# Retention by chunks of 64 tokens in every block, with two 64x64 products per output, in a retention-plus-maxout kernel on one core

## The chip, the cores and the metric

The kernel runs on one core of a Trainium2 chip. The core has a matrix engine (TensorE, PE in the profile; its weight loads are listed apart as PEld), VectorE (DVE), ScalarE (ACT), GpSimd (POOL) and the queue SP, which here issues nearly all DMAs. The engines run on their own and wait for each other by semaphores. The metric is the device time of one execution in microseconds; lower is better. The kernel before was timed three times: 755.7, 756.7 and 758.22 us, a median of 756.7 us.

## The reference

Two stages. The first is a causal retention over 8 batches, 8 heads, 576 tokens and 64 values per head; the second a feed-forward with three up-projections, of which the elementwise largest is kept, and one down-projection.

```python
scores = scale * np.matmul(q, k.transpose(0, 1, 3, 2))          # scale = 1/sqrt(64)
gamma = 1.0 - 2.0 ** (-5.0 - np.arange(H))
Dmat = np.where(rel >= 0, gamma ** rel, 0.0)                    # rel = query position - key position
attn = np.matmul(scores * Dmat, v)                              # (8, 8, 576, 64), per batch and head
x = attn.transpose(0, 2, 1, 3).reshape(4608, 512)
h = np.maximum(np.maximum(x @ w1, x @ w2), x @ w3)              # (4608, 768)
out = h @ w_out                                                 # (4608, 512), float32
```

q, k and v are float32; the four weights arrive as float64 and the kernel turns them into float32 itself.

## The kernel before, in words

The 4608 tokens are 36 *blocks* of 128 tokens (g = 0..35), and four blocks make a *tile* of 512 tokens (t = 0..8). While the feed-forward of tile t runs on TensorE, the retention of the four blocks of tile t+1 is put between its matmuls. A block has two *chunks* of 64 tokens; a batch has nine chunks (`place(g, c)` is 0 to 8).

Because gamma^(i-j) = gamma^i * gamma^-j, the decay is split: keys or values are multiplied by gamma^-j (`gk`), outputs by gamma^i/8 (`gq`), and what older tokens contribute is kept as a *state*, the sum of k^T v over them, multiplied by `gs` = gamma^128 from block to block.

*Blocks 0 to 7 (`BY_CHUNKS = 8`)* are done 128 tokens at once. `transposes` makes q^T and k^T (blocks 0 to 6 on TensorE, L285, with one ACT copy of 128x512 each, L286; block 7 on VectorE). `decay` multiplies v by `gk` on GpSimd into `vd` (L253). `scores` forms 8 products of 64 rows against 128x128 outputs (L299) and masks them with two DVE products (L302, reported as L198). `state` forms k^T v (L366) and `keep` adds it to the state. `values` forms 8 products of scores with values over 128 rows (L407) and 8 of state with q over 64 rows (L420), and `output` multiplies by `gq` into `xT`.

*Blocks 8 to 35* are done by chunks. `chunk_scores` forms, per head, up to four 64x64 products, one in each quadrant of the matrix engine: k^T v of each chunk (L317) and the scores of each chunk (L321). Scores and state lie stacked over the 128 partitions: for a chunk, `ms` holds the weights in one half and q^T in the other, `vas` holds the values in one half and the state in the other. So `chunk_values` needs one product over 128 rows per head and chunk (L438). For that stacking, the mask is two DVE products of 64x512 (L325, with `gm`, the causal mask times `gk`), half of q^T is copied on ACT (L313), and k is multiplied by `gk` on ACT, eight 128x64 products per block (L257, reported as L186). The new state is added on DVE (`keep_chunk`, L333) and multiplied by `gs` on GpSimd (L335).

*The feed-forward.* Tile 0 is plain: 18 up-projections (`up_plain`, L790, 4 matmuls of 512 columns each) and 24 down matmuls (`downs_plain`, L777). During tile 0 the weights arrive by DMA as 64-bit words and are converted in steps on DVE and ACT (`convert_all`, L637 to L663); one call of `convert(1)` runs one step. The very first up-projection is cut into 384 and 128 columns, so that its first part does not need block 3. Later tiles replace the ups by 20 products of 256 columns over sums of weights and of x (`up`, L766), the downs by 7 (`downs`, L564).

*What orders the work.* Instructions are issued in the order of the program text on each engine. `steps(t)` lists by hand at which of 12 points of a tile which step of which block is issued (`transposes`, `scores`, `decay`, `values`, `load`). From tile 1 on, DVE work is not issued at once but put in `urgent` (by `soon`) and handed out between matmuls by `chore`; ACT's scaling is handed out by `scale`. `scores` and `values` first issue all that is left of these. All loads stand in the one queue SP, in program order, and a load into a buffer waits for the last reader of what the buffer held. PSUM has eight banks: four for retention (`ps_r`, four buffers of one bank), two for `ps_x`, two for `ps_y`.

*The start (L869 to L912).* Blocks 0 to 3 are loaded; between them two small loads of `gs` (L874), and the first weight pieces behind block 3's q. Then transposes, scores, state and values of blocks 0 to 3 are issued one after the other, and after them the first up-projection.

## Time and profile before

| | |
|---|---|
| median of the three timed runs | 756.7 us |
| the profiled execution | 756.22 us |
| its span, first to last instruction | 754.5 us |
| PE busy | 745.1 us (99%) |
| DVE busy | 529.2 us (70%) |
| ACT busy | 336.3 us (45%) |
| POOL busy | 90.9 us (12%) |
| granted TensorE clock, mean | 1.000 |
| first up-projection starts | 25.36 us |
| tile 0 runs on PE (up and down) | 25.36 to 125.10 us |
| one later tile, from `e` to the next `e` | 208.57 to 287.37 us |

In the profile's tables a row names the line, the engine, the operation, output and inputs, their shapes, how often it occurs, busy time and the mean of one instruction. Matmuls overlap: the mean of one is not the time that a further one costs. What a stretch of matmuls costs is read from the timeline, from its first start to the start of what follows. Each float32 product appears as two records. A few records can be missing from a trace.

### The profile page before, as it was taken

To read this page: it belongs to the slowest core of one execution; us is meant where nothing else is said; L and a number is where in the kernel's file an instruction comes from. 1 tells how busy PE (TensorE), PEld (TensorE's weight loads), DVE (VectorE), ACT (ScalarE), POOL (GpSimd) and SP (SyncE) were. 2 spreads that over 40 slices of the span, in tenths; PEclk is the share of its full clock that TensorE was granted. 3 is DMA by queue.
4 is the path that set the end of the run, shared out by engine and by line. 5 is a ranking of instruction groups with operands and counts; after the bars stand their busy time and mean duration, and the time that the engine had idled before them with its cause. 6 is when DMAs were issued, how large, how long until landed. Compare 5 with 4: busy or idle time off the path is not lost.

```text
span 754.5 us, 15014 instructions
## 1 busy us (share of the span) xinstructions
PE 745.1 (99%) x5928; PEld 607.9 (81%) x5928; DVE 529.2 (70%) x879; ACT 336.3 (45%) x670; POOL 90.9 (12%) x112
## 2 busy tenths in 40 slices
PE   8999999999999999999999999999999999999998
PEld 7645545588888888888888888888888888888887
DVE  2998796958886866687567847685768666863662
ACT  3665531155245533553355435542555255414441
POOL 3210012002010110011010102010101010100000
PEclk9999999999999999999999999999999999999999
DMA  9995762504242414242343225242425141000001
GB/s 211 229 244 121 201 140 68 102 1 75 67 101 41 85 43 102 54 74 54 71 85 65 62 60 95 38 77 63 82 40 98 43 91 37 1 30 28 2 1 56
DMA packets 230310, 59.20 MB, mean 78 GB/s; under 512 B 211168, under 2 KB 228960, under 8 KB 230240
## 3 DMA queue, kind: packets, MB, share of 16 engines
q1 hardware_dynamic: 229664, 57.91, 35.5%
q8 instruction: 46, 0.75, 0.4%
q10 hardware_dynamic: 576, 0.33, 0.2%
q14 instruction: 24, 0.20, 0.1%
HBM read 48.76 MB, written 9.44 MB: 77 GB/s over the span
## 4 chain that ended last, share of the span: by engine, by line
PE 89%; DVE 5%; DMA 3%; SPq 1%; issue 1%; ACT 1%; DVEq 0%
PE a L766 18%; PE b L766 15%; PE dx L564 11%; PE c L766 8%; PE up L790 6%; PE dz L564 5%; PE d L766 5%; PE e L766 5%; PE o L438 4%; PE sk L317 3%; PE dy L564 3%; PE down L777 2%; DMA bits<-in_moe_w_out_dram 1%; PE sk L321 1%; SPq L247 1%
## 5 line engine op out<-in xcount | busy, mean ns | idle before, releaser
L754 DVE TENSOR_TENSOR part<-part 128x512 f32<-128x512 f32 x161 | 111.4, 692 | 93.6 <-ACT part L751 91.2
L751 ACT COPY part<-b 128x512 f32<-128x512 f32 x115 | 67.3, 585 | 140.2 <-PE b L766 140.2
L754 DVE TENSOR_TENSOR h<-h,part 128x512 f32<-128x512 f32 x115 | 79.6, 692 | 28.8 <-ACT h L751 24.6
L790 PE MATMUL up<-xT,w 128*128 128x512 f32 (+2 forms) x200 | 84.8, 579 | 1.0 <-DVE w L663 0.9
L751 ACT COPY part<-a 128x512 f32<-128x512 f32 x92 | 53.9, 585 | 48.9 <-PE a L766 48.4
L790 PEld LDWEIGHTS up<-xT,w 128*128 128x128 f32 x200 | 36.8, 190 | 43.3 <-issue 40.1
L766 PE MATMUL a<-s,w 128*128 128x256 f32 x276 | 70.9, 379 | 0.0
L766 PE MATMUL b<-s,n 128*128 128x256 f32 x276 | 70.8, 379 | 0.0
L186 ACT ACTIVATE kraw<-kraw,gk 128x64 f32<-128x64 f32 x208 | 65.6, 346 | 3.2 <-DMA kraw<-in_k_dram 2.9
L766 PEld LDWEIGHTS b<-s,n 128*128 128x128 f32 x276 | 52.4, 190 | 7.1
L766 PEld LDWEIGHTS a<-s,w 128*128 128x128 f32 x276 | 52.4, 190 | 7.2
L534 POOL TENSOR_TENSOR H<-h 128x256 f32<-128x256 f32 x24 | 20.2, 842 | 285.6 <-DVE h L754 285.5
L335 POOL TENSOR_TENSOR va<-va,gs_of 64x512 f32<-64x512 f32 x24 | 25.8, 1074 | 229.8 <-DVE va L333 184.2
L766 PE MATMUL c<-xT,w 128*128 128x256 f32 x184 | 49.1, 389 | 0.0
L766 PE MATMUL d<-s,w 128*128 128x256 f32 x184 | 47.3, 379 | 0.0
L766 PE MATMUL b<-xT,n 128*128 128x256 f32 x184 | 47.2, 379 | 0.0
L564 PE MATMUL dx<-To,H 128*128 128x256 f32 (+1 forms) x204 | 44.9, 370 | 0.0
L766 PE MATMUL e<-xT,w 128*128 128x256 f32 x184 | 43.5, 379 | 0.0
L766 PE MATMUL a<-xT,n 128*128 128x256 f32 x184 | 43.5, 379 | 0.0
L564 PEld LDWEIGHTS dx<-To,H 128*128 128x128 f32 x204 | 36.6, 190 | 4.9
L325 DVE TENSOR_TENSOR m<-sk,gm 64x512 f32<-64x512 f32 x56 | 38.5, 687 | 1.0
L766 PEld LDWEIGHTS e<-xT,w 128*128 128x128 f32 x184 | 35.0, 190 | 5.2 <-DVE va L331 0.2
(122 smaller groups left out, 1318.1 us busy)
## 6 DMA issues: line engine op xcount, KB each, us to landing
bits<-in_moe_w_dram SPq DMA_DIRECT2D x36, 256.0 KB, 5.5
out_dram<-osb SPq DMA_DIRECT2D x35, 256.0 KB, 2.1
kraw<-in_k_dram SPq DMA_DIRECT2D x32, 256.0 KB, 3.1
qraw<-in_q_dram SPq DMA_DIRECT2D x224, 32.0 KB, 2.2
kxraw<-in_k_dram SPq DMA_DIRECT2D x224, 32.0 KB, 2.1
va<-in_v_dram SPq DMA_DIRECT2D x56, 128.0 KB, 3.1
bits<-in_moe_w_out_dram SPq DMA_DIRECT2D x6, 512.0 KB, 6.3
vraw<-in_v_dram SPq DMA_DIRECT2D x7, 256.0 KB, 4.5
```

What stands on the lines that cost most here:

```text
L186: scaling.popleft()()
L317: nc.tensor.matmul(sk[c][half(c), h, :], lhsT=kr[half(c), h, :], rhs=vas[g, c][half(c), h, :], start=True, stop=True)
L325: nc.vector.tensor_tensor(ms[g, c][half(c)], sk[1 - c][half(c)], gm[half(c)], op=ALU.mult)
L335: nc.gpsimd.tensor_tensor(to[half(1)], to[half(1)], gs_of[half(1)].unsqueeze(2).to_broadcast([D, H, D]), op=ALU.mult)
L438: nc.tensor.matmul(o[half(c), n % 2, n // 2, half(m)], lhsT=vas[g, m][:, h, :], rhs=ms[g, m][:, h, :], start=m == 0 and n == 0, stop=True, ...
L534: urgent.append(lambda: (pool(s3, a11, a21, op=ALU.subtract), pool(s4, a12, s2, op=ALU.subtract)))
L564: nc.tensor.matmul(o, lhsT=hS[n](fp)[:, m * P:(m + 1) * P], rhs=late["T"][n][:, fp, cols], start=first and fp == order[0] and (m == 0 or l ...
L751: nc.scalar.copy(of[step], ps[step[0]][:])
L754: nc.vector.tensor_tensor(of[dst], a, b, op=op)
L766: nc.tensor.matmul(ps[chain][:, e, :], lhsT=factor(w, 2 * fp + e), rhs=xS[t][x], start=n == 1 and e == 0, stop=ends, skip_group_check=True)
L777: nc.tensor.matmul(b[:], lhsT=h[:, fb, m * P:(m + 1) * P], rhs=w_sb["out", fb], start=(fb == 0), stop=(fb == NF - 1))
L790: nc.tensor.matmul(ps[:, cols], lhsT=w_sb[i, fb][:, dc * P:(dc + 1) * P], rhs=xT[t][:, dc, cols], start=dc == 0 and cols.start == 0, stop= ...
```

## The change

Every block is done by chunks, and the stacked form is given up.

- `transposes` writes q^T and k^T so that chunk c lies in half c of the partitions. For blocks 0 to 6 (still transposed on TensorE) this takes four ACT copies of 64x256 per tensor instead of one of 128x512.
- `decay` multiplies v in place by `gk`: on VectorE for blocks 0 to 3, on GpSimd for the others until tile 1, then on ACT in eight pieces. k is not multiplied any more, and the mask is the bare causal mask, applied by one DVE product of 128x512 per block.
- `scores` forms scores and k^T v as before per head in four 64x64 quadrants, now into one tile of two PSUM banks: the scores of both chunks in the first, k^T v in the second. `keep_chunk` adds the states, one 64x512 DVE product per chunk.
- `values` takes two 64-row products per head and chunk, weights with values and then state with q^T, in the order (rows 0, out 0), (1, 1), (0, 1), (1, 0), which add up in PSUM. A pair of blocks shares one output tile of two banks.
- `ps_r` becomes two buffers of two banks. The helpers for blocks 0 to 7 (`state`, `keep`, `output`, `carry`, `state_factors`, `key_masks`) go, as does ACT's copy of half of q^T.
- The start: `gs` is loaded from ACT's queue ahead of everything else, `gq` in four DMAs on ACT's queue instead of two; the first weight pieces are loaded ahead of block 3. Blocks 0 to 2 are done first; `first_ups` runs the first up-projection over blocks 0 to 2 and the second over blocks 0 and 1, and does scores and values of block 3 between these parts. The transposes and scores of block 4 come one step later than before. In the last unit of tile 0 the maximum is issued ahead of the conversion steps.
- `FILL`, an unused tile, goes from 160 to 192 bytes per partition.

```diff
-    ps_r = ctx.enter_context(tc.tile_pool(name="ps_r", bufs=4, space=PSUM))
+    ps_r = ctx.enter_context(tc.tile_pool(name="ps_r", bufs=2, space=PSUM))
...
     nc.scalar.dma_start(gk[:], key_decay)
+    for j in range(2):
+        nc.scalar.dma_start(gs[0:D, j::2].unsqueeze(2), state_decay[D * j:D * (j + 1), :, D * j:D * j + 1])
...
-    def decay(g):
+    def decay(g, engine=nc.gpsimd):
+        t = vs[g]
         if spread:
+            scaling.extend(partial(nc.scalar.mul, t[:, h, :], t[:, h, :], gk[:, h:h + 1]) for h in range(H))
         else:
+            engine.tensor_tensor(t[:], t[:], gk[:].unsqueeze(2).to_broadcast([C, H, D]), op=ALU.mult)
...
+        for e, (n, src) in enumerate((("k", raws["k", g]), ("q", raws.pop(("q", g))))):
...
             for p in range(NP):
                 nc.tensor.transpose(pt[:, p, :], pair(src, p), ident[:C, :C])
-            nc.scalar.copy(both[n][:], pt[:])
+            for j in range(2):
+                for c in range(2):
+                    nc.scalar.copy(both[n][half(c), j::2, :], pt[half(j), :, half(c)])
...
     def scores(g):
         chore(len(urgent))
         scale(len(scaling))
+        qT, kT, kr = qks[g]["q"], qks[g]["k"], raws.pop(("k", g))
+        sk = ps_r.tile([P, 2, H, D], FP32, tag="r", name="sk")
+        kept = [c for c in range(2) if place(g, c) < CS - 1]
         for h in range(H):
             for c in range(2):
+                nc.tensor.matmul(sk[half(c), 0, h, :], lhsT=kT[half(c), h, :], rhs=qT[half(c), h, :],
                                  start=True, stop=True)
+            for c in kept:
+                nc.tensor.matmul(sk[half(1 - c), 1, h, :], lhsT=kr[half(c), h, :], rhs=vs[g][half(c), h, :],
+                                 start=True, stop=True)
+
+        def mask():
+            nc.vector.tensor_tensor(weights[g][:], sk[:, 0], lower, op=ALU.mult)
+
+        def keep_chunk(c):
+            r = half(1 - c)
+            new, kv = states[g + c][r], sk[r, 1]
+            factor = gs[r].unsqueeze(2).to_broadcast([D, H, D])
+            if place(g, c) > 0:
+                nc.vector.tensor_tensor(new, kv, states[g][half(c)], op=ALU.add)
+                if c:
+                    nc.gpsimd.tensor_tensor(new, new, factor, op=ALU.mult)
...
-    def values(chunks, new_states=(), later=False):
+    def values(chunks):
         chore(len(urgent))
         t, i = divmod(chunks[0], CPT)
+        o = ps_r.tile([P, 2, 2, NP, D], FP32, tag="r", name="o")
+        for n, g in enumerate(chunks):
+            for u in range(NP):
+                for m, c in ((0, 0), (1, 1), (0, 1), (1, 0)):
+                    h = head(c, u)
+                    nc.tensor.matmul(o[half(c), m, n, u, :], lhsT=vs[g][half(m), h, :],
+                                     rhs=weights[g][half(m), h, :],
+                                     start=n == 0 and u == 0, stop=place(g, m) == 0, skip_group_check=True)
+        for n, g in enumerate(chunks):
+            for u in range(NP):
+                for m, c in ((0, 0), (1, 1), (0, 1), (1, 0)):
+                    h = head(c, u)
+                    if place(g, m) > 0:
+                        nc.tensor.matmul(o[half(c), m, n, u, :], lhsT=states[g][half(m), h, :],
+                                         rhs=qks[g]["q"][half(m), h, :], start=False, stop=True, skip_group_check=True)
...
+    def first_ups(h):
+        g = CPT - 1
+        *rest0, copy0 = up_plain(0, h, 0, 0, g * C)
+        convert(3)
+        decay(g, nc.vector)
+        convert(1)
+        scores(g)
+        convert(2)
+        more, *rest1, copy1 = up_plain(0, h, 1, 0, (g - 1) * C, g * C)
+        values([g])
+        for step in (more, *rest0, copy0, *rest1, copy1):
+            step()
+        convert(8)
...
     warm(6)
-    for g in range(CPT):
+    for g in range(CPT - 1):
         load(g)
-        if g == 1:
-            for j in range(2):
-                nc.sync.dma_start(gs[half(j)].unsqueeze(2), state_decay[half(j), :, D * j:D * j + 1])
     load_weights(1)
+    load(CPT - 1, "kq")
+    load_weights(1)
+    load(CPT - 1, "v")
+    load_weights(2)
     load(CPT)
-    load_weights(4)
-    decay(0)
-    key_masks()
+    load_weights(2)
     transposes(0)
     for c in range(2):
-        of_rows = out_decay[:, NP // 2 * c:NP // 2 * (c + 1), :].rearrange("(b p) u c -> p b (u c)", b=2)
-        nc.scalar.dma_start(gq[half(c)].rearrange("p b u c -> p b (u c)"), of_rows)
+        for j in range(2):
+            nc.scalar.dma_start(gq[half(c), j::2, :], out_decay[half(j), NP // 2 * c:NP // 2 * (c + 1), :])
+    decay(0, nc.vector)
     warm(2)
     scores(0)
     transposes(1)
+    decay(1, nc.vector)
+    values([0])
     scores(1)
+    values([1])
     transposes(2)
+    decay(2, nc.vector)
+    scores(2)
+    convert(3)
+    values([2])
+    convert(1)
     transposes(3)
...
-            at(1, (scores, a), (state, a), (keep, a))
-            at(2, (transposes, b), (decay, b), (load, c))
+            at(1, (transposes, a), (decay, a))
+            at(2, (scores, a), (transposes, b), (decay, b), (load, c))
             at(3, (scores, b), (load_blocks, d, 0))
```

## The prediction

> **What bounds the kernel now.** I read the page's head first, then TensorE's waits, then the timeline of TensorE around the retention steps, and last the stretches of tile 0.
>
> ```profile
> span 754.5 us, 15014 instructions
> PE 745.1 (99%) x5928; PEld 607.9 (81%) x5928; DVE 529.2 (70%) x879; ACT 336.3 (45%) x670; POOL 90.9 (12%) x112
> ...
> L754 DVE TENSOR_TENSOR part<-part 128x512 f32<-128x512 f32 x161 | 111.4, 692 | 93.6 <-ACT part L751 91.2
> ...
> L325 DVE TENSOR_TENSOR m<-sk,gm 64x512 f32<-64x512 f32 x56 | 38.5, 687 | 1.0
> ```
>
> TensorE is busy for 99% of the span. DVE idles 93.6 us ahead of one group alone, so its work in the later tiles is not on the path. The waits say where TensorE does stand still:
>
> ```profile
> PE o L407 <- POOL vd L253: 1.6, 1, 1.6
> PE warm L150 <- POOL ident masks.py:199: 1.4, 1, 1.4
> PE sk L321 <- DVE m L191: 0.9, 1, 0.9
> PE up L790 <- DVE w L663: 0.9, 1, 0.9
> ...
> PE down L777 <- DVE h L794: 0.3, 1, 0.3
> ```
>
> Some 6 us in all, and after 26 us only 2.1. So from there the time is the sum of what TensorE issues. What one retention step costs there is read from start to next start:
>
> ```profile
> 234.19 2.08 PE L438 MATMUL o<-m,va 128*64 128x64 f32 x64
> 236.21 1.13 PE L766 MATMUL c<-xT,w 128*128 128x256 f32 x4
> ...
> 253.67 0.27 PE L317 MATMUL sk<-va,kraw 64*64 64x64 f32 x2
> 253.69 0.27 PE L321 MATMUL sk<-m,kT 64*64 64x64 f32 x2
> ...
> 255.70 1.13 PE L766 MATMUL c<-xT,w 128*128 128x256 f32 x4
> ```
>
> The values of a pair of blocks, 32 products over 128 rows, take 2.02 us; its scores and states, 64 products in four quadrants, 2.03 us. Four 64x64 products thus cost about what two of 128x64 do. Blocks 4 to 7 are dearer (chain of work, start and length):
>
> ```profile
> 66.09 1.90 PE o L407 x32
> 67.99 0.93 PE kv L366 x32
> 68.92 0.84 PE o L420 x32
> ...
> 114.80 1.90 PE o L407 x32
> 116.70 0.47 PE kv L366 x16
> 117.16 1.03 PE o L420 x32
> ```
>
> The last view is of tile 0 in stretches (columns: PE, PEld, DVE, ACT, POOL busy):
>
> ```profile
> 26.00:35.00 9.00, 9.00 (x63) 5.75 (x61) 8.01 (x16) 7.10 (x11) 1.92 (x2) 1.00 1.11 254
> 45.00:55.00 10.00, 10.00 (x38) 4.78 (x37) 9.33 (x12) 4.72 (x4) 0.68 (x1) 1.00 1.09 249
> 55.00:65.00 10.00, 10.00 (x24) 4.37 (x23) 9.72 (x12) 6.72 (x7) 0.36 (x1) 1.00 0.72 179
> 65.00:75.00 10.00, 10.00 (x112) 6.06 (x111) 6.65 (x9) 3.57 (x3) 0.93 (x1) 1.00 0.36 77
> ```
>
> While the weights are converted, DVE is as full as TensorE, save for a wait of 3.0 us for values at 66.8 us and one of 3.2 us for weights at 85 us.
>
> **The sum.** The profiled execution took 756.2 us (span 754.5, 1.7 around it); the median is 0.5 higher, and I add that at the end.
>
> *Blocks 8 to 35, 14 pairs.* Scores keep their products and quadrant order: 0. Values go from 32 products to 64 (less 8 for each of six chunks that begin a batch). They have the shape and order of today's scores, so I price them by that row: 2.03 - 2.02, 0.0 to 0.1 us in all. Bounds: if first chunks shorten their rounds, 6 x 0.23 = -1.4 us (a chunk's four rounds of state products are a quarter of half of 2 us); by the other 64-row row, L420, 16 products in 0.84 to 1.03 us, a pair would take 3.4 to 4.1, at most +29 us. L420 has wider outputs, so the score row is nearest.
>
> *Blocks 4 to 7, inside tile 0.* Values, states and old states of blocks 4 and 5: 3.67 -> 2.03. Blocks 6 and 7: 3.40 -> 2.03. Block 4's state, 34.43 to 35.04, goes: 0.61. Scores: 1.09 for one block (L299), about 1.05 after: -0.1. Together -3.7 us.
>
> *Block 3.* It is finished before 25.36 now and comes after the first matmul then: half a pair of each kind, +2.0 us.
>
> *The start.* Today the first up starts at 25.36, 0.06 after DVE wrote its weight. Then, step by step:
> - Key and query copies are 64x256; the 128x256 ACT copy takes 0.372, successive ones start some 0.1 earlier than the end, so four take 1.2 and eight 2.3 us, against 1.1. L347's 0.40 is the other end (+0.2 per block).
> - ACT's queue then holds four `gq` issues of 0.65 us, the last behind block 1's v (used by POOL at 9.76). So block 1's copies start at 10.4 and end at 12.7 (10.1 now). `gq` itself lands 3.3 later, at 13 to 14, and DVE's first output, with mask 1 behind it, waits for that.
> - Scores 1 end at 13.5, mask 1 at 14.4, values 1 at 15.6; transposes 2 and eight copies to 18.4; scores 2 at 19.2. On DVE mask 2 and two states at 0.6 each (an instruction of 0.69 us starts 0.60 after the one before: four masks of L198 took 2.48), then exponent, fraction, mantissa, two outputs, sign and product to 24.4.
> With 0.05 per handover over a dozen handovers: first up at 25.1, -0.3 us. Bounds 24.2 (no handover cost) and 26.5 (`gq` a microsecond late and copies at 0.40).
> - Behind it the second weight (about 29) holds the second up for some 0.4 us, and block 4's eight copies, queued behind three conversions on ACT, hold its scores for 0.6. Two waits go: 0.9 at 43.9 (the weight is there) and 0.3 at 103 (the last maximum no longer stands behind two conversion steps). Sum -0.2; bounds -1.2 (no new hold) to +1.5 (each new hold a microsecond longer or so).
>
> *DVE in tile 0.* Per block one mask of 0.6 instead of two, but two states of 0.6 instead of one of 0.33, and block 3 and its decay now fall in this stretch: +2.9 us. The cover is the 3.0 us wait at 66.8, of which the shorter TensorE work leaves about half, and the wait at 85. I take 0.3 of stall; with the cover gone, +2.9.
>
> *Priced at nothing.* Masks in later tiles (56 x 0.687 become 28 x 0.69) and ACT's copies of q (28 x 0.61): DVE and ACT idle there. GpSimd's factors keep their number. SP loses the two `gs` issues (1.8 us), 16 of block 7's 32 small loads and 28 v loads; each v buffer is now held until the values have read it, as the stacked one was. Behind such a load stand output stores, with two buffers each; nothing on TensorE reads them. If SP runs earlier or later, the 0.9 wait at 174 (q of block 9) goes or doubles: 0 taken, -0.9 to +0.9. The PSUM ring holds the same three tenants (output, two scores) in the same eight banks.
>
> Sum: 0.1 - 3.7 + 2.0 - 0.3 - 0.2 + 0.3 = **-1.8 us**, 754.4 in the profiled frame, 754.9 at the median; I say 754.7 since the holds at the first ups are rounded up.
>
> **A rule against the change.** Today each row half writes a bank of its own (`sk0`, `sk1`); afterwards both write bank 0 for scores and bank 1 for states, in different partition halves. No row here shows that. The Trainium skill, "TensorEngine Tiling (Array Packing)", Gotcha 1, says that different row tiles cannot access one PSUM bank simultaneously; "PSUM — Partial Sum Buffer", on bank collisions, narrows measured collisions to the same bank and the same 32 partitions. By the first, a row half would wait for the other and the sum would be that of rival 3; by the second it stays as it is. I take the second because the two halves here never meet in a partition.
>
> **The rivals.**
> 1. *The start is not later and the ups hide their holds.* For it: DMA of block 2 lands by 13 us, the weight piece is issued some 4 us sooner. Against: the copies on ACT. First up at 24.2 and no new hold: 754.9 - 0.9 - 1.0 - 0.3 = 752.7.
> 2. *The other side: the conversion stretch becomes bound by DVE and ACT.* The place is 26 to 66 us, where DVE is 89 to 97% busy. For it: +2.9 on DVE, and 3 blocks x 1.2 on ACT, of which conversion waits. Against: the wait at 66.8. If both sit on the path, TensorE's saved 2.3 us up to block 5 are worthless: -1.8 + 2.9 + 3.6 - 0.3 = +4.4, 761; with half of it +1.3, 758. It decides once 1.8 us of these 6.5 are exposed beyond the 0.3 already in the sum.
> 3. *Quadrants lose their overlap* (row halves in one bank, or accumulation): a round of scores doubles, 18 pairs x 2 us = +36, some 791. For it: no row with this layout. Against: column halves share a bank at full rate in L407 and L366.
> 4. *The change does not do what it says*, the split products costing as L420 does: +20 to +29, near 780. Against: same shape as L317.
>
> **Chances.** Likeliest, -1.8: 0.52, own range 753.2 to 756.3. Rival 1: 0.18. Rival 2: 0.24. Rivals 3 and 4: 0.06. 0.3% (2.3 us) is about what a measurement of this kernel tells from no change, so the bounds are 754.4 and 759.0. The likeliest case gives 0.24 faster, 0.28 same; rival 1 0.18 faster; rival 2 0.08 same, 0.16 slower; the last two slower: 0.42, 0.36, 0.22. The range 752.3 to 759.5 leaves out rivals 3 and 4, a third of rival 2 and the ends of rival 1.
>
> **What would show it.** Right: values of a pair take 2.0 to 2.1 us in later tiles, and a tile still takes 78.8; the first up starts at 24 to 26.5 us; values of blocks 4 and 5 take about 2.0; tile 0's last down ends 1 to 3 us before 125.1. Wrong in the start: first up after 27. Wrong in the cover: TensorE waits for a weight or a maximum of more than 1.5 us in tile 0. Wrong in the price: later tiles of 82 us or more, or below 78.

## The result

The changed kernel takes 779.1 us (median of four, 776.3 to 780.2), the kernel before beside it 756.2 us: a ratio of 1.029, with a 95% interval of 1.026 to 1.033. It is slower by 22.9 us, where I had forecast 2 us less. The profiled execution took 780.23 us.

The head of the page of the kernel after and its row of the granted clock (40 equal slices, tenths of full speed):

```profile
span 778.3 us, 17555 instructions
...
PE 751.8 (97%) x7224; PEld 611.4 (79%) x7224; DVE 519.1 (67%) x854; ACT 330.9 (43%) x680; POOL 81.8 (11%) x97
...
PEclk9679999999999999999999999999999999999999
```

DVE, ACT and GpSimd are busy for less time than before; TensorE has lost two points of its share, and its clock, 1.00 throughout in the kernel before, dips in the second and third slice. The whole loss lies ahead of tile 1, which begins at 148.79 us instead of 125.10; from there to the end both take the same (629.5 and 629.4 us).

The values of one pair in a later tile and those of blocks 4 and 5 (timeline of TensorE after; start, length, number of records):

```profile
257.99 1.16 PE L309 MATMUL o<-m,vraw 64*64 64x64 f32 x64
258.97 1.11 PE L317 MATMUL o<-qT,state 64*64 64x64 f32 x48
260.01 1.13 PE L634 MATMUL c<-xT,w 128*128 128x256 f32 x4
...
87.44 1.16 PE L309 MATMUL o<-m,vraw 64*64 64x64 f32 x64
88.42 1.11 PE L317 MATMUL o<-qT,state 64*64 64x64 f32 x48
89.46 2.84 PE L658 MATMUL up<-xT,w 128*128 128x512 f32 x6
```

From start to next start both take 2.02 us, as the stacked products did, and less than the 3.67 us of blocks 4 and 5 before. The products were priced right. The waits of TensorE were not (in total, how often, the longest):

```profile
PE kqt L246 <- ACT kT L249: 11.3, 3, 8.1
PE sk L262 <- ACT qT L249: 2.7, 2, 1.6
PE up L658 <- DVE w L531: 2.1, 1, 2.1
PE o L309 <- DVE m L269: 2.1, 2, 1.3
PE down L645 <- DVE w_out L531: 2.0, 1, 2.0
```

The first row is new: TensorE, transposing q of blocks 4, 5 and 6, waits for ACT to copy k. In the timeline of TensorE it looks like this:

```profile
30.12 5.46 PE L658 MATMUL up<-xT,w 128*128 128x384 f32 x8 [2.09 <-DVE w L531]
...
43.23 0.60 PE L246 MATMUL kqt<-ident,kraw 128*128 128x128 f32 x4
51.90 1.12 PE L246 MATMUL kqt<-ident,qraw 128*128 128x128 f32 x4 [8.07 <-ACT kT L249]
52.80 8.75 PE L658 MATMUL up<-xT,w 128*128 128x512 f32 x16
...
64.82 0.66 PE L246 MATMUL kqt<-ident,qraw 128*128 128x128 f32 x4 [1.59 <-ACT kT L249]
...
124.16 15.70 PE L645 MATMUL down<-w_out,h 128*128 128x512 f32 x32 [2.05 <-DVE w_out L531]
```

and on ACT at the same time:

```profile
45.94 1.21 ACT L507 ACTIVATE mant<-bits,one 128x1024 f32<-128x1024 uint32 x1
48.12 1.15 ACT L513 ACTIVATE expo<-expo,top 128x1024 f32<-128x1024 int32 x1 [0.97 <-DVE expo L505]
49.30 1.15 ACT L516 ACTIVATE expo<-expo,inf 128x1024 int32<-128x1024 f32 x1
50.36 1.49 ACT L249 COPY kT<-kqt 64x256 f32<-64x256 f32 x4
53.05 1.54 ACT L249 COPY qT<-kqt 64x256 f32<-64x256 f32 x4 [1.21 <-PE kqt L246]
```

For blocks 4 to 6 both tensors are transposed into one tile of two banks (`kqt`). Its second half is written after copies of its first half were issued, so the transposes of q stand behind the copies of k, and these stand on ACT behind three conversions. TensorE, whose matmuls run in the order of the program, idles for 8.07 us with ups behind it. In the kernel before, where k and q have a tile each, q's transposes follow those of k at once, though block 4's copies start only at 31.86 us:

```profile
28.93 0.60 PE L285 MATMUL kt<-ident,kraw 128*128 128x128 f32 x4
29.37 0.60 PE L285 MATMUL qt<-ident,qraw 128*128 128x128 f32 x4
...
43.94 7.13 PE L790 MATMUL up<-xT,w 128*128 128x512 f32 x16 [0.89 <-DVE w L663]
```

The last view is of stretches of the kernel after (length, then busy PE, PEld, DVE, ACT, POOL; then the granted clock, DMA's share and GB/s):

```profile
20.00:30.00 10.00, 6.41 (x136) 5.29 (x136) 6.36 (x11) 6.24 (x15) 1.28 (x1) 0.61 0.98 219
30.00:36.00 6.00, 5.88 (x32) 3.02 (x36) 3.32 (x6) 3.32 (x6) 0.00 (x0) 0.52 0.73 182
...
44.00:52.00 8.00, 0.10 (x1) 0.11 (x2) 7.28 (x11) 6.77 (x11) 0.00 (x0) 0.63 0.48 123
```

The clock is at half speed from 22 to 35 us, and again around the long wait. So the first part of the first up took 5.46 us, where the same part takes 2.8 at full clock in runs below, two ups took 8.75 instead of 7.1, and the first 16 down matmuls (32 records) 15.70 instead of some 14.1.

Four marks on TensorE's timeline divide the loss: first up, the up behind block 5's transposes (four ups done and block 4 scored, in both), first down, first up of tile 1.

| | first up | behind block 5's transposes | first down | tile 1 | span |
|---|---|---|---|---|---|
| before | 25.36 | 43.94 | 100.31 | 125.10 | 754.5 |
| after | 30.12 | 65.31 | 124.16 | 148.79 | 778.3 |

To the first up 4.8 us are lost, in the second stretch 16.6, in the third 2.5, in the last nothing. The second stretch has 8.07 and 1.59 of waits for the copies of k, 2.7 and 1.7 by the clock in the ups, 2.3 for scores and values of block 3, 0.5 of wait for `xT`, and some 1.3 because transposes ran slower and the first ups are cut into more parts. Against these stand 1.5 that went: block 4's own state products (0.6) and a wait of 0.9 for a weight.

### The profile page after: what moved, and what is told of

Read it like the earlier page. It is cut to its first block, busy times and chain, and to the rows that moved or that the text cites. A ratio compares the mean times of both kernels' runs of the same rounds, so it can differ in the third digit from the quotient of the medians.

```text
span 778.3 us, 17555 instructions
## 1 busy us (share of the span) xinstructions
PE 751.8 (97%) x7224; PEld 611.4 (79%) x7224; DVE 519.1 (67%) x854; ACT 330.9 (43%) x680; POOL 81.8 (11%) x97
## 4 chain that ended last, share of the span: by engine, by line
PE 90%; ACT 3%; DVE 3%; SPq 2%; DMA 1%; issue 1%; ACTq 0%; POOL 0%; DVEq 0%; POOLq 0%
PE a L634 18%; PE b L634 15%; PE dx L432 11%; PE c L634 8%; PE up L658 8%; PE dz L432 5%; PE d L634 5%; PE e L634 5%; PE sk L262 3%; PE down L645 3%; PE dy L432 3%; PE o L309 2%; PE o L317 2%; SPq L202 1%; ACT kT L249 1%
## 5 line engine op out<-in xcount | busy, mean ns | idle before, releaser
L658 PE MATMUL up<-xT,w 128*128 128x512 f32 (+3 forms) x216 | 89.8, 572 | 2.6 <-DVE w L531 2.1
L658 PEld LDWEIGHTS up<-xT,w 128*128 128x128 f32 x216 | 40.3, 199 | 45.6 <-issue 43.7
L177 ACT ACTIVATE vraw<-vraw,gk 128x64 f32<-128x64 f32 x208 | 65.6, 347 | 4.1 <-DMA vraw<-in_v_dram 4.1
L279 POOL TENSOR_TENSOR state<-state,gs 64x512 f32<-64x512 f32 x28 | 30.5, 1090 | 299.6 <-DVE state L277 275.5
L262 PEld LDWEIGHTS sk<-qT,kT 64*64 64x64 f32 x1152 | 37.8, 138 | 14.7 <-issue 7.7
L262 PE MATMUL sk<-qT,kT 64*64 64x64 f32 x1152 | 42.1, 224 | 4.3 <-ACT qT L249 2.7
```

Source lines behind the costliest of these rows:

```text
L177: scaling.popleft()()
L262: nc.tensor.matmul(sk[half(c), 0, h, :], lhsT=kT[half(c), h, :], rhs=qT[half(c), h, :], start=True, stop=True)
L279: nc.gpsimd.tensor_tensor(new, new, factor, op=ALU.mult)
L658: nc.tensor.matmul(ps[:, a:b], lhsT=w_sb[i, fb][:, dc * P:(dc + 1) * P], rhs=xT[t][:, dc, a:b], start=dc == 0 and a == 0, stop=dc == NDC - ...
```

## The experiments

Theory A: the order inside `transposes` costs most, 10 to 14 us. Rivals: the copies in quarters cost as such; the half clock (theory C); the order of block 3 and the first ups. The times of the kernel before beside these runs were 755.9 to 757.1 us.

Marks come from one profiled execution each. Runs whose programs are the same up to the first up start it up to 1.5 us apart (28.65 us in run 1 and 30.09 in run 7; 26.95 in run 6 and 25.48 in run 9), so a difference of that size between two starts says nothing by itself.

### 1. All transposes ahead of the copies

```diff
+        pts = []
...
             for p in range(NP):
                 nc.tensor.transpose(pt[:, p, :], pair(src, p), ident[:C, :C])
+            pts.append((n, pt))
+        for n, pt in pts:
             for j in range(2):
                 for c in range(2):
                     nc.scalar.copy(both[n][half(c), j::2, :], pt[half(j), :, half(c)])
```

> The changed kernel with one edit: for every block transposed on TensorE, the eight transposes (four of k, four of q) are issued first and the eight ACT copies behind them. Theory A (the shared two-bank tile makes q's transposes wait for ACT's copies of k, 8.1 us for block 4 and 1.6 each for blocks 5 and 6): these 11.3 us go, and with them the half clock of the matmuls behind the long wait (8.7 instead of 7.1 us for two ups); 12 to 14 us faster than the changed kernel, 765 to 768 us. Theory B (the conversion on DVE and ACT sets the pace of tile 0, and the wait only shows it): the stall comes back as a wait for a weight or a maximum, less than 5 us gained, 774 us or more.

766.6 us, ratio 1.014 (1.011 to 1.017): 12.5 us came back. The row of `kqt` is gone:

```profile
PE up L661 <- DVE w L534: 2.8, 2, 2.1
PE sk L265 <- ACT qT L252: 2.3, 4, 1.6
PE down L648 <- DVE w_out L534: 2.0, 1, 2.0
...
111.40 14.00 PE L648 MATMUL down<-w_out,h 128*128 128x512 f32 x32 [2.04 <-DVE w_out L534]
```

Number and size of the copies are the same as before the edit, so over half of the loss was the order of sixteen instructions in each transposed block. The marks are now 28.65, 54.10, 111.40 and 134.33 us. Between the profiled executions, 14.5 us apart, the second stretch is 9.7 us shorter and the third 1.6. Of the rest, 1.5 us lie ahead of the first up, within the spread of starts, and 1.7 at the downs, which waited as long as before but ran at full clock this time. The later runs build on this one, save the fourth.

### 2. q's copies on DVE at the start

```diff
-                    nc.scalar.copy(both[n][half(c), j::2, :], pt[half(j), :, half(c)])
+                    copy = nc.vector.tensor_copy if n == "q" and g < CPT else nc.scalar.copy
+                    copy(both[n][half(c), j::2, :], pt[half(j), :, half(c)])
```

> As e1_transposes_first, and q's four quarter copies of blocks 0 to 3 run on DVE beside ACT's four of k. Theory A2 (the start is late since eight ACT copies of 0.38 us stand in a row ahead of each block's scores): each of blocks 0 to 2 has its scores some 1.5 us sooner, the first up starts 3 to 5 us before that of e1 and the time falls by as much, 761 to 764 us. Rival (DVE, which then carries mask, states, decay and copies, or the outputs' factor loaded on ACT's queue, sets the start): under 1 us.

767.1 us, 1.014 (1.011 to 1.016): no gain. Scores now wait 3.7 us for DVE's decay of v, and the first up starts at 29.64 us. Relieving ACT loads DVE, which stands on the same chain.

### 3. Block 3 ahead of the first up

```diff
     transposes(3)
+    decay(3, nc.vector)
+    scores(3)
+    convert(2)
+    values([3])
+    convert(2)
...
-                    first_ups(h)
+                    for fb in range(2):
+                        maximum, = up_plain(t, h, fb, i)
+                        convert(5)
+                        maximum()
```

> As e1_transposes_first, but blocks 0 to 3 are all finished before the first up-projection, which is not cut any more (the change's order of the first two products is undone; the conversion steps are as many). If that order is worth what it is written for, this is 1 to 3 us slower than e1. If DVE and ACT are what the first ups wait for anyway, no difference beyond 1 us; if the mask and states of block 3 between the conversion steps hold the second weight, it is faster than e1.

770.0 us, 1.018 (1.014 to 1.021): 3.4 us slower than the first run. The first up starts at 37.95 us. Given this start, the new order of the first ups is worth about 3 us (the four times lie between 766.9 and 771.8, so the size is loose); it is no part of the loss.

### 4. Dummy products in the gaps of the changed kernel

```diff
+            if n == "q" and g == CPT:
+                warm(34)
             for p in range(NP):
                 nc.tensor.transpose(pt[:, p, :], pair(src, p), ident[:C, :C])
...
     decay(2, nc.vector)
+    warm(7)
     scores(2)
+    warm(5)
     convert(3)
     values([2])
     convert(1)
     transposes(3)
+    warm(9)
```

> The changed kernel, untouched but for matmuls on the identity put into TensorE's gaps: 7 and 5 around the scores of block 2, 9 ahead of the first up, 34 between the transposes of k and q of block 4. They compute nothing. Theory C (a part of the loss is TensorE's clock, granted at 0.5 from 22 to 35 us and at 0.63 to 0.79 from 44 to 62 us after gaps): the clock stays at 1.00, the first part of the first up takes 2.7 us instead of 5.5 and the two ups behind the wait 7.1 instead of 8.7; 3 to 6 us faster than the changed kernel, though the waits stay. Rival (the clock only slows what waits anyway): within 1 us.

775.7 us, 1.026 (1.023 to 1.028): some 3.4 us of the 22.9 are the clock by itself. The timeline of TensorE, with the dummies filling a wait and not shortening it:

```profile
31.17 2.85 PE L660 MATMUL up<-xT,w 128*128 128x384 f32 x8 [1.25 <-DVE w L533]
...
42.07 7.76 PE L151 MATMUL warm<-ident 128*128 128x128 f32 x68
50.99 0.66 PE L248 MATMUL kqt<-ident,qraw 128*128 128x128 f32 x4 [1.17 <-ACT kT L251]
51.48 7.03 PE L660 MATMUL up<-xT,w 128*128 128x512 f32 x16
```

The part of the first up takes 2.85 us instead of 5.46, the two ups behind the wait 7.03 instead of 8.75.

### 5. The same dummies on top of the first run

The 7, 5 and 9 dummy products of run 4 at the start, without the 34.

> On top of the run with all transposes ahead of the copies (766.6 us): idle TensorE time at the start is filled with 7 and 5 dummy products around the scores of block 2 and 9 before the first up; no wait is taken away. Theory of the clock (in that run it is 0.5 from 21 to 35 us and the first part of the first up takes 5.46 us instead of 2.65): the part goes back to 2.7 to 2.9 us, the small products to half their length, 763 to 764.5 us. Rival (the start is bound by DVE's chain to the weights, which the clock does not touch, and the second up then waits longer for its weight): 766 to 767.5 us although the part is short.

767.1 us, 1.014 (1.011 to 1.016): no gain. The first part takes 2.85 us behind a wait of 1.24 for its weight, and ups behind it wait 0.40 and 0.43 for theirs. So the time is the rival's, but its cause is not shown. In the profiled execution the gain is there at first: the second mark comes at 52.50 us instead of 54.10, the first down at 109.80 instead of 111.40. It goes in the downs, which behind the same wait of 2.04 us run at half clock here (15.70 us) and at full clock in run 1 (14.00).

### 6. Transposes sooner

```diff
     scores(1)
-    values([1])
     transposes(2)
+    values([1])
     decay(2, nc.vector)
+    convert(2)
     scores(2)
-    convert(3)
-    values([2])
-    convert(1)
     transposes(3)
+    convert(1)
+    values([2])
+    convert(1)
```

> On top of the run with all transposes ahead of the copies: block 2's transposes go ahead of the values of block 1, block 3's ahead of the values of block 2, and two steps of the first weight's conversion go ahead of block 2's mask on DVE. Theory (the start is a chain from transposes over copies, scores and mask to the first weight): block 2's scores start near 17.7 us instead of 19.4, the first weight is ready 1.5 to 3 us sooner (25.5 to 27 us instead of 28.5), and the whole takes 763 to 765 us. Rival (DVE's sum of work sets it): the first up still starts after 28 us and the time stays at 766 to 767.

763.4 us, 1.009 (1.007 to 1.011): 3.2 us better, as the theory of the chain said. First up at 26.95 us and at full clock. Marks: 26.95, 49.47, 107.22, 131.84.

### 7. Scores of block 6 a step sooner

```diff
-            at(7, (transposes, d), (decay, d), (load_blocks, d + 1, 1, 2))
-            at(8, (scores, c), (scores, d), (load_blocks, d + 1, 3), (load, d + 1))
+            at(7, (scores, c), (transposes, d), (decay, d), (load_blocks, d + 1, 1, 2))
+            at(8, (scores, d), (load_blocks, d + 1, 3), (load, d + 1))
```

> On top of the run with all transposes ahead of the copies: the scores, mask and states of block 6 come one step (two ups) sooner than those of block 7, not in the same step, so that less of DVE's work stands right ahead of the first output weight. Theory (the 2.0 us that the downs of tile 0 wait for their weight come from the masks and states of blocks 6 and 7): the wait falls below 1 us, 765 to 766 us. Rival (DVE is full over the whole stretch from 70 us, so that it is late whatever the order): the wait stays at 1.8 to 2.1, time 766 to 767.

768.7 us, 1.016 (1.014 to 1.019): 2 us slower than the first run; the wait of the downs became 2.4 us. A miss for both expectations: the lump was not helped by starting it earlier. How much of the 2 us the edit itself costs is open, since in the profiled execution the first up, ahead of everything it moves, was 1.4 us later.

### 8. All together, output decay on the other queue

The edits of runs 6 and 7; 4, 4 and 10 dummy products ahead of scores 2, ahead of values 2 and behind them; and:

```diff
     for g in range(CPT - 1):
         load(g)
+        if g == 0:
+            for c in range(2):
+                for j in range(2):
+                    nc.sync.dma_start(gq[half(c), j::2, :], out_decay[half(j), NP // 2 * c:NP // 2 * (c + 1), :])
...
     transposes(0)
-    for c in range(2):
-        for j in range(2):
-            nc.scalar.dma_start(gq[half(c), j::2, :], out_decay[half(j), NP // 2 * c:NP // 2 * (c + 1), :])
```

> All three edits together (transposes sooner, dummy products in the gaps at the start, scores of blocks 6 and 7 apart), and the four loads of the output decay put on the other queue of loads, behind block 0, so that block 1's mask does not stand behind an output that waits for them (1.5 us). Theory (what is left of the loss against the kernel before, 10.8 us, is the late first up with its half clock and the wait of the downs): first up at 22.5 to 25 us, its first part 2.7 to 2.9 us, wait of the downs under 1 us, 755 to 758 us, no more than 0.3% from the kernel before. Rival (block 3 behind the first up and DVE's work in tile 0 cost by themselves): the first up comes at 25 but waits for weights and masks grow behind it, and the time stays above 760.

763.9 us, 1.010 (1.008 to 1.012). The first up starts at 24.87 us at full clock, half a microsecond ahead of the kernel before, and the time is no better than run 6: ups of tile 0 wait for weights (1.9 and 0.5 us) and the downs 2.3 us. The early start is not tested alone here, since run 7's edit, which had cost 2 us, is part of it. But most of the lead goes ahead of that edit's place: 2.1 us at the first up, 1.5 at the second mark (48.00 against 49.47), and then an up waits 1.86 us for its weight at 65 us instead of 0.59, with two ups behind it at half clock (8.83 us).

### 9. Conversions ahead of the maxima in the last unit

On top of run 6:

```diff
-                        if (fp, i) == units[-1]:
-                            maximum()
-                            convert(2)
-                        else:
-                            convert(2)
-                            maximum()
+                        convert(2)
+                        maximum()
+                    if (fp, i) == units[-2]:
+                        convert(2)
```

> On top of the run with transposes sooner (763.4 us): in the last unit of tile 0 the conversion steps stand ahead of the maximum on DVE again, as in the kernel before, and two more steps follow the unit before it, ahead of the masks and states of blocks 6 and 7. Theory (the downs' wait of 2.0 us comes from that order, and it costs more than itself, since the first 32 downs then take 15.70 us instead of 14.1 at a clock of 0.83 in 105 to 115 us): the wait goes, the downs take 14.1, and the time falls by 3 to 3.6 us, to 759.5 to 760.5. Rival (the wait moves to the next weight or to the last maximum, as the work of DVE is the same): 762 to 763.5.

766.7 us, 1.013 (1.011 to 1.015): 3 us slower. Waits and timeline of TensorE:

```profile
PE down L648 <- DVE h L666: 3.7, 2, 2.7
...
113.31 13.12 PE L648 MATMUL down<-w_out,h 128*128 128x512 f32 x26 [2.72 <-DVE h L666]
```

The wait for the weight became a longer one for the last maximum. From the second mark to tile 1 this execution is 2.2 us longer than that of run 6; the rest of its loss lies ahead of the edit, where the clock was lower (the first part of the first up took 4.54 us instead of 2.85). The order in the changed kernel was the better one.

### 10. Block 4's copies between the conversions

On top of run 9:

```diff
-        convert(8)
+        convert(2)
+        transposes(CPT)
+        convert(6)
...
-            at(1, (transposes, a), (decay, a))
+            at(1, (decay, a))
```

> On top of the one with the last unit's order: the transposes of block 4 are issued behind the first two ups and their eight copies go on ACT between the second and third of the eight conversion steps there, not behind all of them. Theory (scores of block 4 stand 1.0 us behind these copies, because ACT is full): the wait of the scores near 45 us goes, a further gain of 0.5 to 1 us. Rival (ACT's order is a zero sum: the conversions that now come behind 3.0 us of copies make DVE and then an up wait for a weight): no gain or a loss of up to 2 us, with a wait of an up for a weight between 40 and 60 us.

768.2 us, 1.015 (1.013 to 1.017), 1.5 us worse than run 9. The wait of block 4's scores went, and ups wait 6.3 us for weights in place of 3.1: on ACT, what is put ahead of the conversions delays the weights.

### 11. Everything, once more

Run 10 with the loads of `gq` and the dummy products of run 8.

> Transposes sooner, dummy products in the gaps at the start, the output decay loaded on the other queue, the last unit's order and the copies of block 4 between the conversions. Theory (all that is left of the loss is late work at the start and at the end of tile 0): 755.5 to 758.5, first up near 24.9 us. Rival (with an early first up the ups of 40 to 66 us wait for weights, since the weights' loads, DVE and ACT set the pace there): 758.5 to 762, with 2 us or more of waits of ups for weights.

765.4 us, 1.012 (1.010 to 1.014), with 2.5 us of wait for a weight at 48 us and the 3.7 us for the maxima: 2.8 us better than run 10, and a miss for both expectations in time, though the rival's waits of ups are there.

### 12. Scores of block 7 a step later

On top of run 6, alone:

```diff
-            at(8, (scores, c), (scores, d), (load_blocks, d + 1, 3), (load, d + 1))
-            at(9, (load_blocks, d + 2, 0, 1))
+            at(8, (scores, c), (load_blocks, d + 1, 3), (load, d + 1))
+            at(9, (scores, d), (load_blocks, d + 2, 0, 1))
```

> On top of the run with transposes sooner (763.4 us), alone: the scores, mask and states of block 7 come one step later than those of block 6, behind the last up, so that DVE does them after the first output weight. Theory of place: the first output weight is ready 2 to 2.7 us sooner, the downs do not wait for it (2.0) and run at full clock (14.1 instead of 15.7 us), the second weight is still in time, since the first two of six take 7 us: 759.5 to 760.5 us. Rival (DVE has too much work in tile 0): the wait moves to the second or third output weight or to the last maximum, 762.5 us or more.

761.4 us, 1.005 (1.004 to 1.007), the best so far and not beaten beyond noise by any later run. Marks: 25.82, 48.31, 104.07, 128.72. The first downs run at once and at full clock; the second output weight is 1.46 us late. Half of either expectation. What holds that weight is on DVE, with GpSimd's rows beside it:

```profile
108.56 2.07 DVE L526 SCALAR_TENSOR_TENSOR expo<-bits,expo 128x1024 int32<-128x1024 int32 x1
110.66 1.95 DVE L534 TENSOR_TENSOR w_out<-mant,expo 128x1024 f32<-128x1024 f32 x1
```

```profile
108.08 1.45 POOL L282 TENSOR_TENSOR state<-state,gs 64x512 f32<-64x512 f32 x1 [8.69 <-DVE state L280]
109.50 2.02 POOL L225 TENSOR_TENSOR vraw<-vraw,gk 128x512 f32<-128x512 f32 x1
```

Both DVE instructions take 1.22 or 1.23 us where GpSimd is idle.

### 13. The same with an early start

Run 12 with the loads and dummies of run 8.

> The same, with the output decay loaded on the other queue and dummy products in the gaps at the start, so that the first up starts at 25 us, as in the kernel before, at full clock. Theory (the start's 1.6 us and the place of block 7 are all): 757 to 759 us. Rival (the ups of 40 to 66 us wait for weights whatever the start, since loads, ACT and DVE set their pace): no better than the run without the early start, within 1 us, with waits of ups for weights of 2 us or more.

762.9 us, 1.007 (1.006 to 1.009): no gain. The first up came at 26.35 us in the profiled run, though, later than run 12's 25.82, with TensorE waiting 0.9 us for a load of q. So this was not the start of run 8, and what an early start is worth alone stays open.

### 14. Decay of blocks 6 and 8 on ACT

```diff
+            if g in (6, 8):
+                for h in range(H):
+                    nc.scalar.mul(t[:, h, :], t[:, h, :], gk[:, h:h + 1])
+                return
```

> On top of the run with block 7's scores later (761.35 us): the decay of the values of blocks 6 and 8 is done by ACT, eight products by a column each, not by GpSimd. Theory (DVE's conversions at 60 and at 108 us are stretched by GpSimd running beside them, and the wait of 0.6 us for a weight near 64 and that of 1.5 us for the second output weight stand behind it): the four stretched instructions come down from 1.95 to 2.08 us towards 1.22, at least the second of each pair, both waits halve or go, 759.5 to 760.5 us. Rival (it is a shortage of ACT as much as of DVE, so that ACT's 1.5 us per block come back as a wait of DVE for ACT): 761 to 763.

761.3 us, 1.006 (1.004 to 1.008), unchanged, although the second of each stretched pair fell to 1.23 us and the wait for the second output weight to 0.76 us. What came back was lost ahead of the edit's place: block 5's transposes run at half clock and an up waits 0.44 us at 41 us, so that the second mark comes at 49.66 us instead of 48.31. From there to tile 1 the profiled execution is 0.85 us shorter than that of run 12; the times don't show it.

### 15. One copy per tensor

```diff
-            for j in range(2):
-                for c in range(2):
-                    nc.scalar.copy(both[n][half(c), j::2, :], pt[half(j), :, half(c)])
+            nc.scalar.copy(both[n][:].rearrange("p h d -> p (h d)"), pt.rearrange("p n c -> p (n c)"))
```

> On top of the run with block 7's scores later: each transposed tensor of blocks 0 to 6 is copied by one ACT instruction of 128x512 instead of four of 64x256, which leaves the heads of a pair in the wrong rows, so that the retention of tile 0 and part of tile 1 is not the reference's; number, order and shapes of all products stay. ACT is relieved of about 1.9 us per block. Theory (the start is a chain through these copies, and ACT is full from 40 to 56 us): the scores of blocks 1, 2 and 4 wait 1 us less each, the first up starts 1 to 2 us sooner, 758 to 760 us. Rival (behind the copies stand loads and DVE, which set the same pace): within 1 us of 761.35.

761.2 us, 1.007 (1.005 to 1.008): no gain, the rival. Two copies take about 1.05 us per block instead of some 3.05, and scores then wait for the decay of v, the values of block 1 for their mask behind the load of `gq`, and ups for weights. So the copies in quarters do not decide as such: the first run left them as they were and won 12.5 us, this one removes them and wins nothing. That they cost nothing is not shown. The clock was lower here (0.73 from 20 to 30 us), and the first part of the first up took 4.36 us instead of 2.85; still the second mark was reached as in run 12 (48.21 and 48.31).

### 16 and 17. Only blocks 4 to 35 by chunks

The start of the kernel before (blocks 0 to 3 whole, one copy per tensor, first ups as before) put into run 1, with a copy of the state at the border; run 17 adds the edit of run 12. In part:

```diff
+    def carry(g):
+        old = states[g]
+        states[g] = spool.tile([P, H, D], FP32, tag="state", name="state")
+        for j in range(2):
+            nc.scalar.copy(states[g][half(0), j::2, :], old[half(j)])
...
-            at(1, (transposes, a), (decay, a))
-            at(2, (scores, a), (transposes, b), (decay, b), (load, c))
+            at(1, (scores, a))
+            at(2, (transposes, b), (decay, b), (load, c))
```

> Blocks 0 to 3, the start, the first ups and the order of maxima and conversions as in the kernel before; blocks 4 to 35 as in the changed kernel, with all transposes ahead of the copies; the state that block 4 takes over is copied into the new layout by two ACT copies. Theory (the changed start lost the time, and the products of blocks 4 to 7 are 3.0 us cheaper): first up at 25 to 26 us, first scores of blocks 4 and 5 with their copies on ACT cost 0.5 to 1.5 us of waits, 753.5 to 756 us, no slower than before. Rival (DVE's states and ACT's quarter copies of blocks 4 to 7 take the saving back in tile 0, the downs wait for their weight or the maximum): 756.5 to 760, with 2 us or more of new waits after 40 us.

> The same with the scores of block 7 behind the last up. Theory (masks and states of blocks 6 and 7 in a lump ahead of the first output weight cost a wait of 2 us, as with the changed start): 1.5 to 3 us faster than without, 751.5 to 754.5 us, faster than the kernel before by 0.3% or more. Rival (with conversions ahead of maxima as in the kernel before there is no such wait, and the move only delays the second weight): within 1 us of the other, or slower.

767.2 us, 1.014 (1.012 to 1.015), and 765.3 us, 1.011 (1.009 to 1.012). Run 17 is 1.9 us faster than run 16, as its theory had it; both times lie above both expectations. The start is not a clean copy: the state factors are loaded in two layouts, DMA's share in 10 to 20 us is 1.27 and 1.29 instead of 1.02, q of blocks 2 and 3 lands late, and the first up starts at 27.57 and 29.71 us. So the times don't answer the question, but the stretch from first up to tile 1 does: 109.0 and 103.2 us against 99.7 before, although its products are cheaper. Two waits of the second (17), and the ups behind one of them:

```profile
PE sk L343 <- ACT qT L266: 2.3, 1, 2.3
...
PE down L726 <- DVE w_out L612: 0.9, 1, 0.9
...
42.23 8.83 PE L739 MATMUL up<-xT,w 128*128 128x512 f32 x16
```

The wait for block 4's copies (2.3 us, and 1.0 more inside its scores, which start before the last copies are done), the half clock behind it (1.7), ups waiting for weights (1.7 after the first up) and the downs' wait (0.9) make 7.6 us. Less the 3.0 us that the values save, 0.6 for block 4's state products and 1.2 of waits that the kernel before has in this stretch, that is 2.8 of the 3.5 us by which it is longer; the rest is in pieces of 0.3 and less. In tile 0 of these runs the chunks give a saving on TensorE and take it back on ACT and DVE.

## Why the prediction was wrong

*Later tiles, +0.1.* Right. Values of a pair take 2.02 us, a tile 78.81 us against 78.80. Rivals 3 and 4 are refuted. The rule weighed against the change, Gotcha 1 of "TensorEngine Tiling (Array Packing)" in the Trainium skill, says that different row tiles cannot access one PSUM bank simultaneously. Here two row halves that write one bank in different partition halves ran at the old rate, 2.02 us for a pair's values, and the measurement decides.

*Blocks 4 to 7, -3.7.* Right as a sum on TensorE: values 2.02 and 2.03 us instead of 3.67 and 3.40, and block 4's own state products are gone.

*Block 3, +2.0.* Right in size: its scores and values take 2.3 us after the first up (2.2 in run 12). Run 3 adds that doing it ahead would have cost some 3 more.

*The holds at the first ups, -0.2. This step failed by most: 11.3 us of waits that the sum did not have, and 12.5 us of time in the first run.* I let "block 4's eight copies, queued behind three conversions on ACT, hold its scores for 0.6", with "a microsecond longer or so" as the bound. The queue was read right: the copies do stand behind three conversions. What I missed is that they hold not only the scores. `kqt` is one tile, q's transposes are issued behind copies that read it, and so TensorE, with both ups, stood behind ACT for 8.07 us at block 4 and 1.59 us at each of blocks 5 and 6. Of a moved step I had counted the instructions, and not asked for each which earlier one it now waits for. The first run shows this cause by itself: with all transposes ahead of the copies these waits are gone.

*The start, -0.3.* Failed: the first up came at 30.12 us, outside my bounds of 24.2 to 26.5. I priced eight copies at 2.3 us, letting each start 0.1 ahead of the end of the last; they took some 3.05 (0.37 to 0.38 each, one after the other). At block 0 TensorE waited behind scores that waited for these copies, so block 1's transposes started at 10.0 us and its copies at 11.15, where I had 10.4; `gq`'s last load landed late enough to hold DVE until 15.19; block 2's transposes were issued behind block 1's values, at 17.9. The clock, which I had not considered at all, was low at 8 to 12 us (0.62 and 0.53) and fell to half at 22 us. Run 6 regained 3.2 us by order alone. In runs 2 and 15 relieving ACT's copies did not bring the first up sooner, and other waits, for DVE's decay and mask and for loads, took their place; so no single member of that chain seems to set it.

*DVE in tile 0, +0.3.* Under-priced. The cover did not hold at the end of tile 0: masks and states of blocks 6 and 7 stand ahead of the first output weight, which is 2.05 us late. This is rival 2's sort of loss, at 124 us, not in its place of 26 to 66. Another order moved the wait more than it removed it: to the maxima (run 9) or, shorter, to the next weight (run 12).

Two signs that I had named for being wrong came: the first up after 27 us, and waits of over 1.5 us for a weight (2.09 and 2.05). So the sum failed as a sum: it added TensorE's savings at full price, and its waits as small change. Run 12 shows what is left where the long wait and the order of the start are mended. The first up is 0.5 us later than before, no difference beyond the spread of starts. The second stretch is 3.9 us longer: block 3's 2.2 us, which the sum had set against an earlier start, a wait for `xT` (0.46), a wait of 1.0 for block 4's copies and 1.0 more inside its scores (45.25 to 47.38 us, where 1.09 is usual), some 0.7 for first ups in more parts, less the 1.5 us that went. The rest of tile 0 is only 0.8 us shorter in spite of the 3.0 us saved in values, with waits of 0.57 and 1.46 for weights. So from the first up to tile 1 TensorE waits 3.5 us for ACT and DVE by the profile's table, against 1.2 in the kernel before. In kind these waits are my rival 2, though it shows only once 18 us of other losses are removed. No version of the change beat the kernel before. Whether one could, with loads and conversions of tile 0 planned anew, stays open.

## What to carry to other kernels

When a tile takes two tensors, issue every writer ahead of the first reader (run 1), or give each tensor its own tile, as the kernel before does: an engine that works in order turns a wait for half a tile into a stop of all that is queued behind it. Price a moved step by asking, for each of its instructions, what its engine has queued ahead and what waits behind it. A saving on the busiest engine counts only where the others have slack; read that from the stretch in question, not from the share of the whole run.

## What the runs showed that I had not expected

- *Half clock without a long pause.* In the changed kernel TensorE was 64 to 75% busy from 10 to 30 us, its longest pauses in the ten microseconds ahead of 22 us were 1.29 and 1.61 us, and the granted clock still went to 0.5 from 23 to 35 us. The Trainium skill, "TensorE: Matmul & The Clock Gate", Part 1, tells of a clock that halves after an idle window of about 3.4 us and returns after a busy one. The direction agrees: behind the idle 8.07 us two ups took 8.75 us instead of 7.1. But here shorter pauses were enough, and not always: a wait of 2.04 or 2.05 us ahead of the downs was followed by 15.70 us for them in the changed kernel and in run 6, and by 14.00 in run 1.
- *A filled gap need not be a gain.* Dummy products gained some 3.4 us in the changed kernel. Those of the start gained nothing in run 5, where what the early clock gave was gone again in the downs.
- *ACT copies of 64x256 from PSUM* took 0.37 to 0.38 us each and did not overlap: eight in some 3.05 us. Two of 128x512, the same elements, took about 1.05.
- *DVE beside GpSimd.* Conversions of 128x1024 took 1.93 to 2.12 us instead of 0.69 or 1.22 while GpSimd scaled states and values. "Trainium Architecture — The Big Picture" in the Trainium skill, under what this means for kernel authors, says that only these two engines contend for a port, one locking the other out; the rows agree that they contend. In run 14, with the values' scaling taken off GpSimd, the second of each pair took 1.23 us; the first, still beside a state, stayed at 2.07 and 2.10.
